# First stage of a fused attention and gated feed-forward kernel: merges, sums of squares and weight conversions at other places of a round

## The chip, the core and the metric

One core of one Trainium2 chip runs the whole program. The metric is the device time of one execution in microseconds (us); the kernel before was timed three times, with a median of 698.71 us (697.16 to 699.35). Engine names in the rows: PE is TensorE's matmul side and PEld its weight load, DVE is VectorE, ACT is ScalarE, POOL is GpSimd, and SP is the queue that issues the DMAs.

## What is computed

Causal attention over 4 batches, 12 heads, 448 positions and head size 64, then an RMS norm over the 768 joined channels and a gated feed-forward layer.

```
scores = q @ k.T / sqrt(64), causal mask, softmax over the keys
x      = (softmax @ v), heads side by side: 1792 x 768
xn     = x / sqrt(mean(x*x) + 1e-6) * rms_g
g, val = xn @ w_gate, xn @ w_val            # 768 -> 1536
out    = (g * sigmoid(g) * val) @ w_out     # 1536 -> 768
```

The weights arrive as 64-bit floats (`in_w`, an int64 view), and the kernel makes 32-bit floats of them itself.

## The kernel before, in words

**Tiles and groups.** A tile is a pair of heads of one batch with some of its queries (`UNITS`). Group 0 has 12 tiles of 256 queries (two for each of the six head pairs c), and this stage, from the start to about 69 us, is the one that the change touches. Two tiles of the same c fill one `xr` of 128 x 512.

**The order of work** is written out by hand. Every engine runs its own instructions in program order. The code walks through ticks (`tick`); a step of the schedule runs at each tick, and `post(n, f)` puts f off by n ticks. One round (`round_steps`) has six ticks and belongs to one tile p: scores of tile p+3, products of tile p with its values, then the two halves of the transposes of tile p+1, with two empty ticks between. The table `T` holds the delays: `exp0`, `norm0` and the like. What the steps issue:

- `scores` (L193, PE) into a `s_ps` bank; `softmax` takes the masked maximum from there (L202, DVE, four maxima for a tile, into `sp` and `nm`), three ticks later the exponentials (L205, ACT) and their sums `sm` (L227, ACT), and seven ticks later `norm`: the reciprocal `rs` (L214, DVE) and the four products sp times rs (L210, POOL; on ACT as L208 for the last two tiles of the group). These four are called the norms below.
- `some` transposes the norms' results (L249, PE) into `t_ps` and `x_ps`; the first half is copied to `pt` by ACT (L255), the second by DVE (L253).
- `products` (L275, PE) multiplies `pt` with the values `v_r`; `copy` brings the result to `xr` (L292, DVE).
- When the second tile of a head pair c is done, `square` (L300 on) makes the squares of its `xr`: on POOL through the helper at L103 for c = 0, 1, 2, on ACT (L308) for c = 3 and 4, on DVE (L310) for c = 5. The squares of c = 1 to 4 are then added to `acc` on DVE (L318), put off by `T["acc"]`. `split_x` makes `xh` (L335, ACT) and `xl` (L336, DVE).
- A weight unit of 128 x 768 is loaded (L395), and `convert_ops` puts its parts off from the tick in `CONVERT`: a scaled copy to `w_c` (L414, ACT, `c0`), a multiplication by zero of one half (L415, POOL, `c1`), the **first merge** (L417, DVE, `c20` in this stage), the **second merge** (L419, DVE, `c30`), and a store to DRAM (L421, SP, `c50`). At the tick in `SPLIT`, `split_w` makes `w_h` (L429, ACT) and `wl0`.. ticks later `w_l` (L431, DVE). The conversions come once in two rounds.
- `ffn_part` (L475 to L477, PE) multiplies finished `xh`, `xl` with finished `w_h`, `w_l`, some of it already between the rounds.
- At the end of the stage the squares are summed over the channels (L344, PE), first `acc`, then the squares of c = 5, and `rms_first` makes the scale from them: a square root (L353, ACT), a reciprocal, four diagonal blocks `dg` (L358, DVE), a matmul with ones (L362, PE) and a copy (L363, ACT).

**What waits for what, around the change:** the sum at L318 needs the squares; the maxima of the next tile stand behind it on DVE; the norms on POOL need `rs`, which stands behind those maxima.

In the table, `acc=3` puts the sum three ticks after the squares; conversions start at these ticks:

```
CONVERT = (20, 32, 44, 56, 62, 85)
SPLIT = (33, 45, 57, 70)
```

Of the kernel before, what the change touches and what calls it, by code (L numbers as in the profile page):

```python
# [10 lines left out]
F32 = mybir.dt.float32  # L11
# [11 lines left out]
P = 128  # L23
NP = H // 2
# [3 lines left out]
W = 512  # L28
# [10 lines left out]
        for g in range(NG) for c in range(NP)}  # L39
# [1 line left out]
MASKED = -8.0e9  # L41


T = dict(c0=0, c1=1, c2=4, c20=12, c3=4, c30=13, c26=5, c36=5, c5=6, c50=16, c56=7, exp=1, exp0=3, gt=1, hh=1, hl=4, ws=5, ld2=7,
         ld=4, ld1=11, lv=5, norm0=7, norm1=2, r0=1, acc=3, dg=1, spread=2, r1=5, so=3, wl=2, wl0=7, wl2=5, wl4=1, xl=2, xl0=9)
LOAD = (4, 12, 24, 36, 48, 60, 74, 86)
CONVERT = (20, 32, 44, 56, 62, 85)
SPLIT = (33, 45, 57, 70)

READY_W, READY_X = (45, 57, 68), (40, 52, 64, 76, 87)  # L50
WR = 4
# [11 lines left out]
def attention_ffn(ctx: ExitStack, tc: tile.TileContext, qk0, qk1, qk2, v, v2, w, g, out, out2):  # L63
# [11 lines left out]
    def pool(name, bufs, at=ctx, **kw):  # L75
        return at.enter_context(tc.tile_pool(name=name, bufs=bufs, **kw))
# [6 lines left out]
    ht_p = pool("ht", 4, ffn, side="left")  # L83
    rm_p = pool("rm", 1, ffn, side="left")
# [9 lines left out]
    def bank(tag, bufs=1):  # L94


        return ps.tile([P, W], F32, tag=tag, name=tag + "_ps", bufs=bufs)
# [4 lines left out]
    def pool_op(out_, a, op, b):  # L102
        nc.gpsimd.tensor_tensor(out_, a, b, op=op)  # L103
# [28 lines left out]
    def post(delay, fn):  # L132
        if delay <= 0:
            fn()
        else:
            later.setdefault(now[0] + delay, []).append(fn)
# [7 lines left out]
    xr, xh, xl, acc, xq = {}, {}, {}, {}, {}  # L144
# [6 lines left out]
    def load_qk(p):  # L151
        if p < len(UNITS):
            _, kind, _, _, row, _ = UNITS[p]
            raw_qk[p] = raw.tile([P, 2, W], F32, tag="qk", name="qk_r")
            if kind == 2:
                nc.sync.dma_start(out=raw_qk[p], in_=qk2[row])
            else:
                nc.sync.dma_start(out=raw_qk[p][:, 0], in_=(qk0, qk1)[kind][row])
# [14 lines left out]
    def steps_s(p):  # L173
# [22 lines left out]
        def softmax(e, i, pss):  # L196
            o, wd = bl[i]
            ps, sp = pss[e][:, o: o + wd], pr["sp"][e][:, o: o + wd]
            n = len(bl) * e + i
            nm, sm, rs = (pr[m][:, n: n + 1] for m in ("nm", "sm", "rs"))  # L200
            mk = mask2 if kind == 2 else mask[:, 3 * P - wd:]
            nc.vector.tensor_tensor_reduce(  # L202
                out=sp, in0=ps, in1=mk, scale=nsc, scalar=3.0e38,
                op0=ALU.add, op1=ALU.min, accum_out=nm)
            post(T["exp" if p >= ENDS[0] else "exp0"], lambda: nc.scalar.activation(  # L205
                sp, sp, AF.Exp, bias=nm, scale=-1.0, accum_out=sm))
            if ENDS[0] - 2 <= p < ENDS[1]:
                pr["norms"].append(lambda: nc.scalar.mul(sp, sp, rs))  # L208
            else:
                pr["norms"].append(lambda: nc.gpsimd.tensor_scalar(  # L210
                    sp, sp, rs, 1.0, op0=ALU.mult, op1=ALU.mult))
# [5 lines left out]
        def step():  # L217
# [6 lines left out]
            for e in range(2):  # L224
                for i in range(len(bl)):
                    softmax(e, i, pss)
            post(T["exp" if p >= ENDS[0] else "exp0"], lambda: nc.scalar.activation(  # L227
                pr["sm"][:, :nb], pr["sm"][:, :nb], AF.Identity, bias=tiny))
            post(T["norm1" if kind else "norm0"], norm)
            post(2, lambda: load_qk(p + 4))  # L230
# [68 lines left out]
    def square(b, c):  # L299

        halves = [(0, HX), (HX, XT)] if b == 2 else [(0, W)]
        for j, (lo, hi) in enumerate(halves):
            x = xr[b, c][:, lo: hi]
            sq = rm_p.tile([P, W], F32, tag="sq", name="sq") if c else \
                rm_p.tile([P, W], F32, tag="acc", name="acc", bufs=2)
            sq = sq[:, : hi - lo]
            if b or 2 < c < NP - 1:
                nc.scalar.activation(sq, x, AF.Square)  # L308
            elif c == NP - 1:
                nc.vector.tensor_tensor(sq, x, x, op=ALU.mult)  # L310
            else:
                pool_op(sq, x, ALU.mult, x)
            if c == 0:
                acc[b, j] = sq
            elif b:
                pool_op(acc[b, j], acc[b, j], ALU.add, sq)
            elif c < NP - 1:
                post(T["acc"], lambda: nc.vector.tensor_tensor(acc[0, 0], acc[0, 0], sq, op=ALU.add))  # L318
        if b == 2:
            return  # L320
        if c == NP - 1 and b:
            post(T["r1"], lambda: rms(b, [acc[b, 0]]))
        elif c == NP - 1:
            cols = column_sums(acc[b, 0], None, True)
            post(T["r0"], lambda: rms_first(column_sums(sq, cols, False)))
        waiting.append((b, c))

    def split_x():
        if not waiting:
            return  # L330
        b, c = waiting.pop(0)
        x, gc = xr[b, c], g_sb[:, c: c + 1]
        h = xx_p.tile([P, W], F32R, tag=f"xh{c}", name="xh")
        l = xx_p.tile([P, W], F32R, tag=f"xl{c}", name="xl")
        nc.scalar.mul(h, x, gc)  # L335
        post(T["xl0" if b == 0 and c < NP - 1 else "xl"], lambda: nc.vector.scalar_tensor_tensor(  # L336
            out=l, in0=x, scalar=gc, in1=f32(h), op0=ALU.mult, op1=ALU.subtract))
        xh[b, c], xl[b, c] = h, l

    def column_sums(sq, ps, first):  # L340

        ps = bank("t")[:, : W // P] if first else ps
        for i in range(W // P):
            nc.tensor.matmul(ps[:, i: i + 1], sq[:, P * i: P * (i + 1)], ones[:, :1],  # L344
                             start=first and i == 0, stop=not first, skip_group_check=True)
        return ps

    def rms_first(ps):

        rc = st_p.tile([P, W // P], F32, name="rc", bufs=1)  # L350
        dg = ht_p.tile([P, W], F32, tag="t", name="dg")
        r = rinv[0] = rm_p.tile([P, W], F32, tag="rms", name="rms", bufs=2)
        nc.scalar.activation(rc, ps, AF.Sqrt, bias=eps, scale=1.0 / DM)  # L353

        def diagonal():
            nc.vector.reciprocal(rc, rc)
            for i in range(W // P):
                nc.vector.tensor_scalar_mul(dg[:, P * i: P * (i + 1)], ident, rc[:, i: i + 1])  # L358

        def spread():  # L360
            ps = bank("t")
            nc.tensor.matmul(ps, ones, dg, start=True, stop=True)  # L362
            nc.scalar.copy(r, ps)  # L363

        post(T["dg"], diagonal)
        post(T["spread"], spread)

    def rms(b, parts):

        ps = bank("t")  # L370
        for i, sq in enumerate(parts):
            nc.tensor.matmul(ps, ones, sq, start=(i == 0), stop=(i == len(parts) - 1))
        r = rinv[b] = rm_p.tile([P, W], F32, tag="rms", name="rms", bufs=2)
        nc.scalar.activation(r, ps, AF.Sqrt, bias=eps, scale=1.0 / DM)
        for i in range(W // P):
            sl = slice(i * P, (i + 1) * P)
            post(i if b else 1, lambda sl=sl: nc.vector.reciprocal(r[:, sl], r[:, sl]))
# [46 lines left out]
    def split_w(s):  # L424
        if s < 2 * NU:
            t = wt[s]
            h = ws_p.tile([P, DM], F32R, tag="wh", name="w_h")
            l = ws_p.tile([P, DM], F32R, tag="wl", name="w_l")
            nc.scalar.copy(h, t)  # L429
            if s < NU or s > NU + 2 * NF and s % 2:  # L430
                post(T[("wl0", "wl0", "wl2", "wl2", "wl4")[s] if s < 5 else "wl"], lambda: nc.vector.tensor_tensor(l, t, f32(h), op=ALU.subtract))  # L431
            else:
                post(T["wl"], lambda: pool_op(l, t, ALU.subtract, f32(h)))
            wt[s] = tuple(a.rearrange("p (k m) -> p k m", m=P) for a in (h, l))
            u = s - NU
            if 0 <= u < 2 * NF:
                pair[u % 2] = t
                if u % 2:
                    post(T["ws"], lambda v=u // 2, t0=pair[0], t1=t: quad_sums(v, t0, t1))
# [400 lines left out]
    with tc.manual_schedule():  # L840
# [27 lines left out]

        for fs, at_ in ((load_w, LOAD), (lambda n: convert(n), CONVERT), (split_w, SPLIT)):
            for n, t_ in enumerate(at_):  # L870
# [14 lines left out]
        def convert(s):  # L885
            for d, op in convert_ops(s):
                post(d, op)
# [13 lines left out]
        for s in range(2 * NU):  # L901
# [15 lines left out]
            for k0 in (0, 2, 4):  # L917
# [7 lines left out]
                if i >= 73 and w_ == 0:  # L925
                    split_x()
                if k0 == (0 if s < 3 else 4) and s + 3 >= len(SPLIT):
                    split_w(s + 3)
                if k0 == 4 and s + 5 >= len(CONVERT):
                    convert(s + 5)  # L930
# [127 lines left out]
```

## Time and profile before

| | before |
|---|---|
| median of three runs | 698.71 us (697.16 to 699.35) |
| the profiled execution | 697.85 us, of which the span from first to last instruction is 696.0 us |
| busy share of the span | PE 97%, PEld 79%, DVE 77%, ACT 55%, POOL 43% |
| granted TensorE clock | 0.998 of full speed |

The span is one execution, read engine by engine. A timeline row gives the start, the length, the engine, the line, the operation and its output and input; in square brackets stands how long the engine had been idle before it and who ended that wait. A windows row gives the busy time of each engine in a stretch of the span. Busy times of neighbouring instructions overlap a little at their ends, so the time that an instruction adds to its queue is read from start to start.

### The profile page before, as it was taken

What the parts mean: (1) busy time and instruction counts of PE and PEld (TensorE: products, weight loads), DVE (VectorE), ACT (ScalarE), POOL (GpSimd) and SP (SyncE); (2) the same over time, 40 slices, a digit from 0 to 9 for tenths busy, and PEclk for the clock granted to TensorE, in tenths of its full rate; (3) what the DMA queues carried; (4) which work ended last, traced back from release to release, by engine and by line L of the source; (5) the groups of instructions that cost most, each with busy time, mean ns of one, the idle gap of its engine ahead of it and who ended that gap; (6) DMA issues with size and microseconds to landing.
All of it is one profiled execution on the core that took longest, in us unless ns stands there. A gap on an engine that the chain in (4) does not pass through costs nothing. (4 is left out here: it accounts for less than half of the span.)

```text
span 696.0 us, 11943 instructions
## 1 busy us (share of the span) xinstructions
PE 671.8 (97%) x4122; PEld 551.9 (79%) x4122; DVE 535.3 (77%) x1053; ACT 379.7 (55%) x856; POOL 298.6 (43%) x267
## 2 busy tenths in 40 slices
PE   8788989999999999999999999999899999999997
PEld 6456767777777767777777777888899999999997
DVE  4877989899988577777687878488386768679993
ACT  6885677888887446346354544445333433355550
POOL 4860212131225533756676566563254536312220
PEclk9999999999999999999999999999999999999999
DMA  8655688789879637576757655415457576553541
GB/s 264 201 201 172 189 254 256 218 259 285 258 218 343 228 117 233 169 238 211 266 159 263 198 174 170 153 60 177 156 189 246 172 247 217 200 151 89 168 139 69
DMA packets 71357, 138.82 MB, mean 199 GB/s; under 512 B 7744, under 2 KB 39232, under 8 KB 71296
## 3 DMA queue, kind: packets, MB, share of 16 engines
q1 hardware_dynamic: 71296, 138.05, 61.6%
q8 instruction: 33, 0.54, 0.3%
q14 instruction: 28, 0.23, 0.1%
HBM read 104.21 MB, written 33.82 MB: 198 GB/s over the span
## 5 line engine op out<-in xcount | busy, mean ns | idle before, releaser
L475 PE MATMUL m_ps<-xh,w_h 128*128 128x512 f32 x276 | 117.4, 425 | 2.5 <-DVE t_sb L502 2.5
L210 POOL TENSOR_SCALAR sp<-sp,rs 128x384 f32<-128x384 f32 (+2 forms) x112 | 78.3, 717 | 94.0 <-DVE rs L214 89.4
L205 ACT ACTIVATE sp<-sp,nm 128x384 f32<-128x384 f32 (+3 forms) x168 | 87.2, 521 | 39.6 <-DVE nm L202 39.6
L477 PE MATMUL m_ps<-xh,w_l 128*128 128x512 f32 x276 | 108.4, 393 | 0.0
L476 PE MATMUL m_ps<-xl,w_h 128*128 128x512 f32 x276 | 108.2, 392 | 0.0
L415 POOL TENSOR_SCALAR w<-w 128x768 f32<-128x768 f32 x36 | 38.6, 1073 | 112.5 <-ACT w_c L414 104.5
L103 POOL TENSOR_TENSOR a_l<-w_q,a_h 128x768 fp32r<-128x768 f32 x24 | 47.3, 1971 | 69.7 <-ACT a_h L516 69.6
L275 PEld LDWEIGHTS a_ps<-pt,v_r 128*64 128x64 f32 (+1 forms) x864 | 41.6, 137 | 38.5 <-DVE pt L253 10.9
L275 PE MATMUL a_ps<-pt,v_r 128*64 128x128 f32 (+2 forms) x864 | 60.0, 268 | 10.6 <-DVE pt L253 6.7
L475 PEld LDWEIGHTS m_ps<-xh,w_h 128*128 128x128 f32 x276 | 51.9, 188 | 14.8 <-issue 6.8
L103 POOL TENSOR_TENSOR w_l<-w_r,w_h 128x768 fp32r<-128x768 f32 x30 | 59.6, 1992 | 7.3 <-ACT w_h L429 7.2
L477 PEld LDWEIGHTS m_ps<-xh,w_l 128*128 128x128 f32 x276 | 51.8, 188 | 11.9
L253 DVE COPY pt<-t_ps 128x384 f32<-128x384 f32 (+1 forms) x71 | 42.4, 597 | 23.9 <-PE t_ps L249 23.4
L202 DVE CUSTOM_DVE_ANT_0 sp<-s_ps,mask 128x128 f32<-128x128 f32 (+3 forms) x136 | 49.9, 415 | 12.3 <-PE s_ps L193 11.1
L475 PE MATMUL m_ps<-hh,w_h 128*128 128x512 f32 x144 | 58.6, 407 | 0.0
L476 PEld LDWEIGHTS m_ps<-xl,w_h 128*128 128x128 f32 x276 | 52.2, 189 | 7.6
L477 PE MATMUL m_ps<-hh,w_l 128*128 128x512 f32 x144 | 56.2, 391 | 0.0
L476 PE MATMUL m_ps<-hl,w_h 128*128 128x512 f32 x144 | 56.2, 390 | 0.0
L249 PE MATMUL t_ps<-ident,sp 128*128 128x128 f32 (+1 forms) x309 | 50.1, 275 | 0.1
L249 PEld LDWEIGHTS t_ps<-ident,sp 128*128 128x128 f32 (+1 forms) x309 | 37.8, 137 | 14.3 <-issue 2.1
L193 PE MATMUL s_ps<-qk_r 64*128 64x128 f32 (+3 forms) x296 | 43.3, 421 | 1.7 <-DVE nm L202 1.5
L431 DVE TENSOR_TENSOR w_l<-w_c,w_h 128x768 fp32r<-128x768 f32 x36 | 40.3, 1120 | 3.9 <-ACT w_h L429 3.9
(196 smaller groups left out, 1678.6 us busy)
## 6 DMA issues: line engine op xcount, KB each, us to landing
w<-in_w SPq DMA_DIRECT2D x36, 768.0 KB, 5.1
w<-w_c SPq DMA_DIRECT2D x36, 384.0 KB, 5.7
w_r<-w SPq DMA_DIRECT2D x36, 384.0 KB, 4.8
qk_r<-in_qk SPq DMA_DIRECT2D x48, 256.0 KB, 4.7
qk_r<-in_qk SPq DMA_DIRECT2D x12, 512.0 KB, 5.6
v_r<-in_v SPq DMA_DIRECT2D x12, 448.0 KB, 5.0
v_r<-in_v SPq DMA_DIRECT2D x24, 192.0 KB, 3.4
wy<-w_r SPq DMA_DIRECT2D x24, 192.0 KB, 4.4
```

The costliest lines, as they stand in the source:

```text
L103: nc.gpsimd.tensor_tensor(out_, a, b, op=op)
L193: nc.tensor.matmul(ps, r[:, q0: q0 + nq], r[:, k0: k0 + wd], start=True, stop=True)
L202: nc.vector.tensor_tensor_reduce(out=sp, in0=ps, in1=mk, scale=nsc, scalar=3.0e38, op0=ALU.add, op1=ALU.min, accum_out=nm)
L205: post(T["exp" if p >= ENDS[0] else "exp0"], lambda: nc.scalar.activation(sp, sp, AF.Exp, bias=nm, scale=-1.0, accum_out=sm))
L210: pr["norms"].append(lambda: nc.gpsimd.tensor_scalar(sp, sp, rs, 1.0, op0=ALU.mult, op1=ALU.mult))
L249: nc.tensor.transpose(ps[:kb, at: at + P], pr["sp"][e][:, o + kb * j: o + kb * (j + 1)], ident)
L253: nc.vector.tensor_copy(pt[:kb, :at], ps[:kb, :at])
L275: nc.tensor.matmul(av_ps[e * D: (e + 1) * D, p % 2, q0: q0 + n], raw_v[p][:kb, h, j, e, :], pr["pt", e][:kb, a0: a0 + n], start=(j == 0), ...
L431: post(T[("wl0", "wl0", "wl2", "wl2", "wl4")[s] if s < 5 else "wl"], lambda: nc.vector.tensor_tensor(l, t, f32(h), op=ALU.subtract))
L475: nc.tensor.matmul(ps, wh[:, k, :], mh, start=(first and k == ks[0]), stop=False)
L476: nc.tensor.matmul(ps, wh[:, k, :], ml, start=False, stop=False)
L477: nc.tensor.matmul(ps, wl[:, k, :], mh, start=False, stop=(last and k == 5))
```

## The change

It changes four delays and two lists of ticks in the schedule's tables, the engine of one square, and the pool of one buffer.

```diff
-T = dict(c0=0, c1=1, c2=4, c20=12, c3=4, c30=13, c26=5, c36=5, c5=6, c50=16, c56=7, exp=1, exp0=3, gt=1, hh=1, hl=4, ws=5, ld2=7,
-         ld=4, ld1=11, lv=5, norm0=7, norm1=2, r0=1, acc=3, dg=1, spread=2, r1=5, so=3, wl=2, wl0=7, wl2=5, wl4=1, xl=2, xl0=9)
+T = dict(c0=0, c1=1, c2=4, c20=16, c3=4, c30=18, c26=5, c36=5, c5=6, c50=19, c56=7, exp=1, exp0=3, gt=1, hh=1, hl=4, ws=5, ld2=7,
+         ld=4, ld1=11, lv=5, norm0=7, norm1=2, r0=1, acc=10, dg=1, spread=2, r1=5, so=3, wl=2, wl0=7, wl2=5, wl4=1, xl=2, xl0=9)
-CONVERT = (20, 32, 44, 56, 62, 85)
-SPLIT = (33, 45, 57, 70)
+CONVERT = (14, 26, 38, 50, 62, 85)
+SPLIT = (34, 46, 58, 70)
@@ square
-            if b or 2 < c < NP - 1:
+            if b or c == NP - 2:
                 nc.scalar.activation(sq, x, AF.Square)
@@ rms_first
-        dg = ht_p.tile([P, W], F32, tag="t", name="dg")
+        dg = rm_p.tile([P, W], F32, tag="sq", name="dg")
```

The first merge of a unit moves from tick 12 to tick 16 after its conversion's start, the second from 13 to 18, the store from 16 to 19, and the sum of squares from 3 to 10 ticks after the squares. The first four conversions start six ticks (one round) sooner, three of the splits one tick later. The squares of c = 3 go from ACT to POOL. The diagonal blocks `dg` use the buffer of the squares and no longer one of the four buffers of `ht_p`. TensorE's order is the same, instruction for instruction.

**VectorE, around the sum of squares.** Before, the end of one round and the first maximum of the next tile (w_l is the low part of a weight unit, w_290 and w_383 are raw weight units):

```order
L214 RECIPROCAL rs<-sm 128x4
L292 COPY xr<-a_ps 128x256
L431 TENSOR_TENSOR w_l<-w_c,w_h 128x768
L253 COPY pt<-x_ps 128x384
L318 TENSOR_TENSOR acc<-acc,sq 128x512
L202 ISA sp,nm<-s_ps,mask 128x128
```

After, the same round, from the last maximum of its own tile to the first maximum of the next:

```order
L202 ISA nm 128x1
L318 TENSOR_TENSOR acc<-acc,sq 128x512
L214 RECIPROCAL rs<-sm 128x4
L292 COPY xr<-a_ps 128x256
L431 TENSOR_TENSOR w_l<-w_c,w_h 128x768
L253 COPY pt<-x_ps 128x384
L417 SCALAR_TENSOR_TENSOR w_383<-w_383 128x768
L202 ISA sp,nm<-s_ps,mask 128x128
```

The sum has gone from ahead of a tile's maxima to behind them, and takes the squares of a pair of rounds earlier; the first merge of the next unit has come in ahead of the maxima.

**VectorE, the other round of the pair.** Before, both merges stand side by side:

```order
L214 RECIPROCAL rs<-sm 128x4
L292 COPY xr<-a_ps 128x256
L417 SCALAR_TENSOR_TENSOR w_290<-w_290 128x768
L419 SCALAR_TENSOR_TENSOR w_c<-w_c,w_290 128x768
L253 COPY pt<-x_ps 128x384
L336 SCALAR_TENSOR_TENSOR xl<-xr,g_sb,xh 128x512
```

After, only the second is left there:

```order
L214 RECIPROCAL rs<-sm 128x4
L292 COPY xr<-a_ps 128x256
L419 SCALAR_TENSOR_TENSOR w_c<-w_c,w_383 128x768
L253 COPY pt<-x_ps 128x384
L336 SCALAR_TENSOR_TENSOR xl<-xr,g_sb,xh 128x512
L202 ISA sp,nm<-s_ps,mask 128x128
```

The copy `pt` that TensorE's products wait for has one merge ahead of it in place of two.

**GpSimd, one pair of rounds.** Before (sp_482, sp_536, sp_537, ... are the score blocks of successive tiles, w64 a raw weight unit):

```order
L415 TENSOR_SCALAR w64_383<-w64_383 128x768
L210 TENSOR_SCALAR sp_536<-sp_536,rs_535 128x128
L210 TENSOR_SCALAR sp_536<-sp_536,rs_535 128x256
L210 TENSOR_SCALAR sp_537<-sp_537,rs_535 128x128
L210 TENSOR_SCALAR sp_537<-sp_537,rs_535 128x256
L103 TENSOR_TENSOR sq_634<-xr_557 128x512
L210 TENSOR_SCALAR sp_597<-sp_597,rs_596 128x128
```

After:

```order
L210 TENSOR_SCALAR sp_539<-sp_539,rs_538 128x128
L210 TENSOR_SCALAR sp_539<-sp_539,rs_538 128x256
L210 TENSOR_SCALAR sp_540<-sp_540,rs_538 128x128
L210 TENSOR_SCALAR sp_540<-sp_540,rs_538 128x256
L103 TENSOR_TENSOR sq_636<-xr_560 128x512
L415 TENSOR_SCALAR w64_493<-w64_493 128x768
L210 TENSOR_SCALAR sp_596<-sp_596,rs_595 128x128
```

Before, a square follows one tile's norms and a multiplication of a weight unit the other's; after, both follow the same tile's norms.

On SP the store of a unit (L421) comes one row sooner, ahead of a load of values (L167) in place of behind it.

## Rows read from the trace of the kernel before

**Rows 1.** Busy time by stretch: stretch in us, its length, each engine's busy us (instructions).
```profile
18.75:29.20 10.45, 8.86 (x61) 5.54 (x57) 8.19 (x27) 10.04 (x32) 9.16 (x12) 1.00 0.75 253
29.20:39.32 10.12, 8.12 (x50) 5.30 (x51) 8.10 (x28) 7.45 (x24) 7.86 (x10) 1.00 0.58 192
39.32:49.21 9.89, 8.42 (x53) 5.40 (x52) 8.10 (x28) 7.63 (x25) 7.72 (x10) 1.00 0.57 197
49.21:62.38 13.17, 9.54 (x54) 5.91 (x52) 10.48 (x25) 10.35 (x26) 0.88 (x1) 1.00 0.61 205
...
69.09:160.00 90.91, 87.29 (x442) 66.35 (x441) 84.48 (x158) 71.05 (x171) 19.65 (x18) 1.00 0.77 239
```

**Rows 2.** Timeline of DVE, from one sum of squares to the next.
```profile
28.60 0.69 DVE L318 TENSOR_TENSOR acc<-acc,sq 128x512 f32<-128x512 f32 x1 [1.98 <-POOL sq L103]
29.20 0.28 DVE L202 CUSTOM_DVE_ANT_0 sp<-s_ps,mask 128x128 f32<-128x128 f32 x1
...
30.31 0.17 DVE L214 RECIPROCAL rs<-sm 128x4 f32<-128x4 f32 x1
30.40 0.39 DVE L292 COPY xr<-a_ps 128x256 f32<-128x256 f32 x1
30.71 0.95 DVE L417 SCALAR_TENSOR_TENSOR w<-w 128x768 int32<-128x768 int32 x1
31.70 0.96 DVE L419 SCALAR_TENSOR_TENSOR w_c<-w_c,w 128x768 int32<-128x768 int32 x1
32.57 0.55 DVE L253 COPY pt<-x_ps 128x384 f32<-128x384 f32 x1
33.04 0.84 DVE L336 SCALAR_TENSOR_TENSOR xl<-xr,g_sb,xh 128x512 fp32r<-128x512 f32 x1
33.81 0.28 DVE L202 CUSTOM_DVE_ANT_0 sp<-s_ps,mask 128x128 f32<-128x128 f32 x1
...
35.32 0.94 DVE L431 TENSOR_TENSOR w_l<-w_c,w_h 128x768 fp32r<-128x768 f32 x1
36.18 0.55 DVE L253 COPY pt<-x_ps 128x384 f32<-128x384 f32 x1
38.71 0.69 DVE L318 TENSOR_TENSOR acc<-acc,sq 128x512 f32<-128x512 f32 x1 [1.99 <-POOL sq L103]
```

**Rows 3.** Timeline of POOL in the same pair, and one undisturbed set of norms before it.
```profile
13.83 1.62 POOL L210 TENSOR_SCALAR sp<-sp,rs 128x128 f32<-128x128 f32 x4 [0.97 <-DVE rs L214]
...
30.66 3.57 POOL L210 TENSOR_SCALAR sp<-sp,rs 128x128 f32<-128x128 f32 x4 [2.10 <-DVE rs L214]
34.20 0.89 POOL L415 TENSOR_SCALAR w<-w 128x768 f32<-128x768 f32 x1
35.25 2.42 POOL L210 TENSOR_SCALAR sp<-sp,rs 128x128 f32<-128x128 f32 x4 [0.15 <-DVE rs L214]
37.64 1.04 POOL L103 TENSOR_TENSOR sq<-xr 128x512 f32<-128x512 f32 x1
```

**Rows 4.** Timelines of POOL and DVE at 118 us, where two of these operations meet.
```profile
118.49 1.15 POOL L415 TENSOR_SCALAR w<-w 128x768 f32<-128x768 f32 x1 [2.61 <-ACT w_c L414]
118.82 1.63 DVE L431 TENSOR_TENSOR w_l<-w_c,w_h 128x768 fp32r<-128x768 f32 x1
```

**Rows 5.** Timeline of DVE: one copy ahead of the maxima that start at 18.75 us.
```profile
17.79 0.56 DVE L253 COPY pt<-x_ps 128x384 f32<-128x384 f32 x1 [0.27 <-PE x_ps L249]
```

**Rows 6.** DMA issues at 6, 26 and 44 us: size and us from issue to landing.
```profile
w<-in_w SPq DMA_DIRECT2D x1, 768.0 KB, 5.1
...
v_r<-in_v SPq DMA_DIRECT2D x1, 128.0 KB, 4.2
...
v_r<-in_v SPq DMA_DIRECT2D x1, 128.0 KB, 6.2
```

**Rows 7.** Timeline of DVE at the end of group 0.
```profile
60.87 0.56 DVE L253 COPY pt<-x_ps 128x384 f32<-128x384 f32 x1 [1.77 <-PE x_ps L249]
...
62.38 0.42 DVE L292 COPY xr<-a_ps 128x256 f32<-128x256 f32 x1 [0.30 <-PE a_ps L275]
```

## The prediction, made before the changed kernel ran

> **What bounds the kernel now.** I read busy time by stretch first. Behind 69 us TensorE is busy nearly all the time (87.29 of 90.91 us), while in the stage that the change touches it is not: the three pairs of rounds between 18.75 and 49.21 us take 10.45, 10.12 and 9.89 us, 30.46 together, and no engine's work needs that [rows 1]. The exception is the first of them, where ScalarE is busy for 10.04 us.
>
> Then the timelines of a pair. VectorE stands still for 1.98 and 1.99 us ahead of the sum of squares, until GpSimd's squares are there [rows 2]. GpSimd in turn stands still for 2.10 us ahead of its next norms, until VectorE's reciprocal is there [rows 3]. Together they make a ring: norms 30.66 to 34.20, the multiplication of a unit, norms from 35.25, squares until 38.68 [rows 3], then on VectorE the sum from 38.71, the maxima, the reciprocal, and the next norms. GpSimd's part is 3.57 + 0.89 + 2.42 + 1.04 = 7.92 us, end to end about 8.0; the sum with the maxima (28.60 to 30.31, 1.71) and the step to GpSimd at 30.66 add 2.1. That is the pair's 10.1 us. The reader is to see that the wait is no lack of speed in an engine: the maxima need nothing from the squares and stand behind a sum that does.
>
> **The sum of squares behind the maxima.** It takes 0.60 us from start to start wherever it stands [rows 2], so its own time is no gain. What goes is the ring: the squares that it takes now were made a pair of rounds earlier. The 2.0 us of VectorE and the 2.1 us of GpSimd go together, being one wait seen from both ends. What is late next are the engines' lists, per pair:
>
> - VectorE, start to start [rows 2]: maxima 1.11 twice, reciprocal and copy 0.40 twice, first merge 0.99, second 0.87, `pt` 0.47 twice, `xl` 0.77, `w_l` 0.86, sum 0.60: 8.05 us.
> - TensorE: busy 8.12 and 8.42 us [rows 1]; matmuls that wait inside are counted whole, so this is an upper end.
> - ScalarE: 7.45 and 7.63 us [rows 1].
> - GpSimd: four norms take 1.62 us alone, 2.42 with one two-input VectorE operation right behind the reciprocal (`w_l`), and 3.57 with both merges and `xl` there [rows 3]. Now one merge follows each reciprocal at most, so I take 2.42 twice: 2 x 2.42 + 0.89 + 1.04 = 6.77. The other end is 3.57 twice, 9.07.
>
> **The two merges apart.** Their 0.99 and 0.87 us stay in VectorE's list. The copy `pt` that releases TensorE's products has one merge less ahead of it. In return the first merge now starts in the middle of a set of norms, and the second near the squares. What such a meeting costs is seen once outside the stage: GpSimd's 1.15 us multiplication had started at 118.49, and VectorE's `w_l`, begun at 118.82, took 1.63 us in place of 0.94 [rows 2, 4], so 0.69 more. In the stage itself `xl` runs beside the norms that are there now and takes 0.84, which is counted above. Two or three of the five two-input operations of a pair will meet something; the norms are short. Bounds: 0, and 0.69 for each of five, 3.45. I take 0.4 to 0.5, nearest to the rows of the stage itself, and so **8.5 us for a pair**, just above TensorE's 8.42.
>
> Three pairs: 30.46 - 25.5 = **5.0 us won**. At VectorE's bare 8.05 it would be 6.3.
>
> **Start of the stage.** The conversions begin a round sooner. The first merge now stands behind the copy of 17.79 [rows 5] and ahead of the maxima that started at 18.75; 0.4 us of its 0.95 fit into VectorE's wait there, and the rest delays those maxima: 17.79 + 0.47 + 0.95 = 19.2. **Cost 0.4 us.** ScalarE's scaled copy of the first unit comes before the third tile's exponentials now. The load takes 5.1 us [rows 6], and its lead is a round shorter now, so ScalarE may stand there for some tenths. Bounds 0 and 0.95, a pass over the same block by VectorE [rows 2]; I take 0, since the first tiles' other work there waits for loads of values anyway, and keep 0.95 for the range.
>
> **End of the stage**, 49.21 to 62.38 us. One first merge (0.99) leaves this stretch for the one ahead of it, and one sum (0.60) comes in later than before, behind `xl` and before the last copy of `xr`. VectorE waits here for TensorE's transposes (1.77) and products (0.30) [rows 7], which themselves wait for copies behind merges, so an earlier merge is felt; ScalarE, busy 10.35 of 13.17 us [rows 1], keeps it from more. Bounds 0 and 1.4 (0.99 and a part of the waits); I take **0.9 won**.
>
> **Other edits.** The squares of c = 3 add 1.04 us to GpSimd [rows 3] where it does next to nothing afterwards (0.88 us of work in 49.21 to 62.38 [rows 1]), since the last two tiles' norms are ScalarE's; covered, 0. If GpSimd should be late there, the sum behind `xl` would wait up to those 1.04. `dg` in the squares' buffer must wait until TensorE has read the squares of c = 5; its own input comes from that very product, so 0. On SP, a load of values is now queued behind a store that waits for the second merge. In the list above that merge ends 6.7 us after the pair's first maximum (1.11 + 0.60 + 0.40 + 0.86 + 0.47 + 0.9 + 1.11 + 0.40 + 0.87), and the products that need these values come behind the next pair's first `pt`, at 8.5 + 3.4, which leaves about 5 us; loads of values took 4.2 us, and 6.2 right behind a 768 KB weight load [rows 6], which now comes after them. I take 0.
>
> **Carrying on.** Every engine works in order, and behind 69 us TensorE is the limit; the rest of the program moves forward as a block. The sum: 5.0 - 0.4 + 0.9 = 5.5 us, from the profiled 697.85 to 692.35. That execution was 0.86 us below the median of the runs, so **693.2 us** for the median.
>
> **Rivals.**
> (a) *GpSimd becomes the bound.* If both sets of norms are held as long as the worst is now, its list is 9.07 us, without any idle time. For: 3.57 is what three held norms cost [rows 3]. Against: only one merge follows each reciprocal now. Three pairs 27.2, won 3.3, less 0.4 at the start: 695.8 for the median. Chance 0.15.
> (b) *The gain is eaten by a late load of values.* If loads behind the store take 6.2 us, products wait 1.2 us in each pair and the first waits more; with GpSimd or ScalarE late as well (10.04 of 10.45 us busy in the first pair [rows 1]), a pair is back near 9.9. Won 0.8 in three, less 0.4 at the start, and nothing at the end: about 698.3. Chance 0.11. That the edits do not move the wait at all belongs here, 0.02 more; the new order speaks against it.
> (c) *Slower: VectorE is held by GpSimd.* In the old order VectorE's two-input operations start right behind the reciprocal, as GpSimd's norms begin, and win. In the new one they start while GpSimd is at work. If each of the five in a pair loses 0.69 us [rows 4], the list is 8.05 + 3.45 = 11.5, 1.35 more than now, 4.0 in three pairs, and with 0.4 at the start the median is about 703. It decides from (10.15 - 8.05) / 5 = 0.42 us for each operation. Against: eight of GpSimd's ten operations in a pair are norms of 0.4 us each (1.62 for four [rows 3]), and a chance meeting costs about half of one. Chance 0.06. The Trainium skill, "SBUF — State Buffer", section "SBUF: two separate sides", says that VectorE, with two SBUF inputs, and a GpSimd operation that reads SBUF share a port pair under an exclusive lock: who starts first has it for the whole instruction, and the other is blocked. The meeting at 118 us agrees with that, the loser there being VectorE.
>
> **Chances and range.** The forecast (pairs of 8.05 to 8.8 us) has 0.66. A difference of 0.3%, 2.1 us, is about what a measurement of this kernel can tell from none, so faster means under 696.6. Forecast and (a) lie there: with a little of (b), 0.82. The same: 0.12. Slower: 0.06. Low end: 8.05 a pair (6.3) with the whole 1.4 at the end and 0.4 at the start give 7.3, 691.4, and 0.4 less if the start costs nothing: 691.0. High end: through (a), with 0.95 more for ScalarE at the start: 696.8. What is left out is (c) and most of (b).
>
> **What would show it.** Right: no idle time of note ahead of the sum of squares; sets of maxima two rounds apart by 8.0 to 8.8 us; GpSimd's 2.10 us before a set of norms gone; the last copy of `xr` near 57 us; the stretches behind 69 us as long as now. Wrong: VectorE's merges, `w_l` or `xl` at 1.3 us and more (c); sets of norms at 3.5 us and GpSimd without idle time (a); TensorE's products released by a DMA (b); or a shorter stage followed by new idle time of TensorE.

## The result, and the profile after

| | before | after |
|---|---|---|
| median, four runs each | 698.91 us (697.16 to 699.35) | 691.64 us (689.42 to 692.87) |
| ratio, 95% interval | | 0.9897 [0.9864, 0.9930] |
| once more, nine runs and five | 698.43 us | 689.92 us, 0.9891 [0.9871, 0.9911] |
| profiled execution, its span | 697.85, 696.0 us | 690.72, 688.9 us |

The changed kernel is 7.3 us faster in the first comparison, 8.5 in the second. The forecast was 693.2, from 691.0 to 696.8: the first median lies inside, the repeat 1.1 us below the low end.

Busy time by stretch of the kernel after: the three pairs of rounds from the first maxima, the end of group 0 up to the last copy of `xr`, then the stretch behind the stage. Columns are those of [rows 1].

```profile
19.21:27.59 8.38, 6.90 (x45) 3.66 (x45) 8.12 (x27) 8.17 (x29) 7.71 (x11) 1.00 0.62 200
27.59:36.11 8.52, 7.89 (x52) 4.73 (x51) 8.52 (x28) 7.44 (x25) 7.72 (x11) 1.00 0.78 277
36.11:44.32 8.21, 7.83 (x55) 5.28 (x54) 8.21 (x28) 6.90 (x23) 8.21 (x11) 1.00 0.67 222
44.32:57.09 12.77, 10.50 (x61) 6.98 (x60) 10.87 (x26) 10.98 (x28) 4.53 (x5) 1.00 0.63 208
65.44:160.00 94.56, 90.88 (x460) 69.11 (x458) 88.06 (x161) 74.25 (x177) 20.89 (x19) 1.00 0.78 237
```

Pairs that took 10.45, 10.12 and 9.89 us [rows 1] take 8.38, 8.52 and 8.21, with VectorE busy without a gap in the second and third. Its timeline in the kernel after, for the counterpart of [rows 2]:

```profile
28.70 0.17 DVE L214 RECIPROCAL rs<-sm 128x4 f32<-128x4 f32 x1
28.79 0.39 DVE L292 COPY xr<-a_ps 128x256 f32<-128x256 f32 x1
29.10 1.08 DVE L419 SCALAR_TENSOR_TENSOR w_c<-w_c,w 128x768 int32<-128x768 int32 x1
30.10 0.55 DVE L253 COPY pt<-x_ps 128x384 f32<-128x384 f32 x1
30.57 0.91 DVE L336 SCALAR_TENSOR_TENSOR xl<-xr,g_sb,xh 128x512 fp32r<-128x512 f32 x1
...
32.51 1.00 DVE L318 TENSOR_TENSOR acc<-acc,sq 128x512 f32<-128x512 f32 x1
...
33.83 0.94 DVE L431 TENSOR_TENSOR w_l<-w_c,w_h 128x768 fp32r<-128x768 f32 x1
34.70 0.54 DVE L253 COPY pt<-x_ps 128x384 f32<-128x384 f32 x1
35.16 1.02 DVE L417 SCALAR_TENSOR_TENSOR w<-w 128x768 int32<-128x768 int32 x1
```

The sum at 32.51 waits for nothing; the 1.99 us ahead of it are gone. POOL in the same pair, for [rows 3]:

```profile
25.24 3.12 POOL L210 TENSOR_SCALAR sp<-sp,rs 128x128 f32<-128x128 f32 x4 [0.67 <-DVE rs L214]
28.33 1.04 POOL L103 TENSOR_TENSOR sq<-xr 128x512 f32<-128x512 f32 x1
29.34 1.60 POOL L415 TENSOR_SCALAR w<-w 128x768 f32<-128x768 f32 x1
30.90 2.06 POOL L210 TENSOR_SCALAR sp<-sp,rs 128x128 f32<-128x128 f32 x4
33.76 3.12 POOL L210 TENSOR_SCALAR sp<-sp,rs 128x128 f32<-128x128 f32 x4 [0.80 <-PE x_ps L249]
```

Where GpSimd stood 2.10 us for the reciprocal, it now waits 0.67 for it, or 0.80 for TensorE's transposes. One meeting shows: the multiplication at 29.34 starts 0.24 us after VectorE's second merge and takes 1.60 us in place of 0.89 [rows 3]; here GpSimd is the one that is held.

**Where the time went.** The two profiled spans differ by 7.1 us. Cut at four instructions that both have (the first maxima, the last copy of `xr`, the first `gr` at L492, the last output block `ob` at L486):

| stretch | before | after | won |
|---|---|---|---|
| start to first maxima | 18.75 | 19.21 | -0.46 |
| to the last copy of `xr` | 43.63 | 37.88 | 5.75 |
| to the first `gr` | 6.71 | 8.35 | -1.64 |
| to the last `ob` | 419.86 | 420.17 | -0.31 |
| to the end | 207.05 | 203.29 | 3.76 |

Two large rows of this table were not in the prediction's sum, the third and the last. The third first; the timeline of all engines of after, end of the stage:

```profile
55.15 0.74 DVE L336 SCALAR_TENSOR_TENSOR xl<-xr,g_sb,xh 128x512 fp32r<-128x512 f32 x1
55.44 1.18 POOL L415 TENSOR_SCALAR w<-w 128x768 f32<-128x768 f32 x1 [7.78 <-ACT w_c L414]
55.81 1.35 DVE L318 TENSOR_TENSOR acc<-acc,sq 128x512 f32<-128x512 f32 x1
57.09 0.41 DVE L292 COPY xr<-a_ps 128x256 f32<-128x256 f32 x1
57.31 1.02 PE L344 MATMUL t_ps<-ones,acc 128*128 128x1 f32 x8 [1.15 <-DVE acc L318]
...
61.83 2.02 PE L362 MATMUL t_ps<-dg,ones 128*128 128x512 f32 x2
65.44 0.69 DVE L492 TENSOR_TENSOR gr<-m_ps,rms 128x512 f32<-128x512 f32 x1 [1.93 <-PE m_ps L477]
```

The last sum, of c = 4, now stands just ahead of the last copy of `xr`, meets a GpSimd multiplication, and takes 1.35 us in place of 0.69. TensorE's column sums (L344) wait 1.15 us for it; in e3 and e5 below the sum stands at the same place, nothing holds it (0.68 us), and they wait 0.60 and 0.61. Three microseconds after the wait the clock falls; the stretch in a windows view of after:

```profile
60.60:64.00 3.40, 3.40 (x7) 1.79 (x6) 2.74 (x6) 0.12 (x1) 0.00 (x0) 0.50 0.01 2
```

The granted clock is 0.50, 1.2 in place of 2.4 GHz, for 3.4 us, so about 1.7 us of work are lost; the matmul with ones at 61.83 takes 2.02 us, where it takes 1.10 at full clock. From the column sums to the first `gr` it is 8.13 us here, 7.10 in e9 below, whose clock stays at 1.00, and 6.81 before: about 1.0 us of the row goes with the clock. Before the fall TensorE had waited those 1.15 us and worked on from 57.31. In the profile of the kernel before the same stage has no such stretch; it has one elsewhere, which leads to the last row of the table. The timeline of before behind its last `ob`, and the window that follows:

```profile
488.95 0.69 DVE L486 SCALAR_TENSOR_TENSOR ob<-m_ps,rms 128x512 f32<-128x512 f32 x1 [4.33 <-PE m_ps L477]
490.50 0.43 SPq L488 DMA_DIRECT2D out_t<-ob  x1
494.05 0.48 ACT L648 COPY m<-m_ps 128x384 f32<-128x384 f32 x1 [4.77 <-DMA out_t<-ob]
494.58 0.44 PE L625 MATMUL m_ps<-ch,a_h 128*128 128x384 f32 x1 [2.54 <-ACT m L648]
```

```profile
495.80:499.20 3.40, 3.40 (x13) 3.40 (x12) 2.41 (x2) 2.70 (x4) 1.97 (x2) 0.50 0.26 62
```

The same place in after:

```profile
485.61 0.69 DVE L486 SCALAR_TENSOR_TENSOR ob<-m_ps,rms 128x512 f32<-128x512 f32 x1 [4.55 <-PE m_ps L477]
487.17 0.43 SPq L488 DMA_DIRECT2D out_t<-ob  x1
487.18 0.48 ACT L648 COPY m<-m_ps 128x384 f32<-128x384 f32 x1 [1.24 <-PE m_ps L625]
491.11 0.56 DVE L653 TENSOR_TENSOR u<-m,s_ps 128x384 f32<-128x384 f32 x1 [4.34 <-ACT t L662]
```

L648 is the first copy of the second feed-forward part (`m1`, in a pool that is opened when those of the first part are closed, so in their memory). Before, it waited until the last output block had been stored, TensorE waited 2.54 us for the copy, and in this execution the clock fell to 0.50 behind that (e2 below has the same wait without the fall). After, the copy waits for TensorE alone. ScalarE's order of instructions is the same at this place; the semaphores that the copy waits for are not. Before, then after:

```order
L648 COPY m_5643<-m_ps 128x384 [waits DMAHW0_49,DVE_49,PE_49]
```

```order
L648 COPY m_5643<-m_ps 128x384 [waits DMAHW3_49,PE_49]
```

So the memory that `m1` takes over belonged to the last `ob` before, and to an earlier one now. What shifted it: `dg` no longer takes one of the four buffers "t" of `ht_p`, in which `gr`, `ob` and others go round. With one user fewer ahead of them, each later one lies one buffer further back.

### The profile page after: what moved, and what is told of

Same layout as the page of the kernel before. It is cut to its first block, busy times and chain, and to the rows that moved or that the text cites. A ratio compares the mean times of both kernels' runs of the same rounds, so it can differ in the third digit from the quotient of the medians.

```text
span 688.9 us, 11941 instructions
## 1 busy us (share of the span) xinstructions
PE 671.3 (97%) x4122; PEld 551.2 (80%) x4122; DVE 536.5 (78%) x1053; ACT 378.2 (55%) x855; POOL 301.0 (44%) x268
## 5 line engine op out<-in xcount | busy, mean ns | idle before, releaser
L415 POOL TENSOR_SCALAR w<-w 128x768 f32<-128x768 f32 x36 | 41.1, 1143 | 109.9 <-ACT w_c L414 101.8
```

## The experiments

Theory: the gain in the stage (5.35 us in its three pairs) comes from the sums behind the maxima, and the gain behind 485 us from `dg` alone. Rivals: that the new places of merges and conversions make the gain, or that it is one effect carried along. In the table, "first `gr`" and "tail" (last `ob` to end) come from each kernel's one profiled execution, "clock" is the mean granted clock over its timed runs.

| run | median us | ratio [95%] | first `gr` | tail | clock |
|---|---|---|---|---|---|
| e1_dg | 695.18 | 0.9961 [0.9945, 0.9977] | 70.38 | 204.5 | 0.994 |
| e2_nodg | 693.10 | 0.9929 [0.9906, 0.9952] | 65.08 | 206.5 | 0.997 |
| e3_acc | 694.54 | 0.9953 [0.9932, 0.9974] | 65.87 | 206.2 | 0.996 |
| e4_noacc | 696.94 | 0.9969 [0.9951, 0.9988] | 72.14 | 206.0 | 0.994 |
| e5_acc_dg | 691.19 | 0.9902 [0.9885, 0.9918] | 64.84 | 203.6 | 0.998 |
| e6_lastob | 690.71 | 0.9893 [0.9875, 0.9911] | 65.07 | 204.8 | 0.997 |
| e7_c4early | 687.79 | 0.9856 [0.9837, 0.9876] | 62.33 | 204.0 | 1.000 |
| e8_after | 689.92 | 0.9891 [0.9871, 0.9911] | 64.67 | 203.1 | 0.997 |
| e9_c4early | 689.50 | 0.9879 [0.9857, 0.9900] | 62.54 | 205.5 | 1.000 |
| e10_sqact | 688.93 | 0.9872 [0.9852, 0.9892] | 62.66 | 202.4 | 1.000 |
| e11_short | 689.66 | 0.9886 [0.9868, 0.9904] | 64.90 | 203.1 | 1.000 |
| e12_pair | 693.67 | 0.9945 [0.9925, 0.9965] | 66.60 | 206.1 | 0.998 |

The kernel before had 698.53 beside the first four, 698.43 beside the next four, 697.54 beside the last, and a mean clock of 0.994 in these 46 runs.

### `dg` alone (e1), and everything but `dg` (e2)

```diff
# e1: the kernel before with
-        dg = ht_p.tile([P, W], F32, tag="t", name="dg")
+        dg = rm_p.tile([P, W], F32, tag="sq", name="dg")
# e2: the changed kernel with that line as before
```

> The kernel before with one edit: the diagonal blocks in the squares' buffer. Theory A (the change has two gains: the ring in the first stage, and this buffer, which shifts the ring of four output buffers by one, so that ScalarE's first copy at the start of the second feed-forward part no longer waits 4.77 us for the last output store): the first stage is as before (last copy of xr near 62.4 us, sum of squares waiting about 2.0 us), TensorE's idle 2.54 us near 494 is gone, and the time is 2.5 to 4.2 us less, 694.7 to 696.4. Rival B (all of the gain is the schedule of the first stage, and what differs near 494 is scatter between executions): no difference from before, 698.9, and the wait of 4.77 us still there.

> The changed kernel with the diagonal blocks back in their old buffer. Theory A: the first stage as in the changed kernel (pairs of 8.2 to 8.6 us), the copy near 488 waits over 4 us for the output store, and the time is 694 to 696. Rival B: 691.6, like the changed kernel.

`dg` alone wins 3.35 us and nothing in the stage (its first `gr` is even later than before, 70.38 against 69.09, in a profile whose clock fell at 54.7 us). The copy of e1:

```profile
491.93 0.48 ACT L648 COPY m<-m_ps 128x384 f32<-128x384 f32 x1 [1.24 <-PE m_ps L625]
496.33 0.55 DVE L653 TENSOR_TENSOR u<-m,s_ps 128x384 f32<-128x384 f32 x1 [4.81 <-DMA out_t<-ob]
```

The wait for the store has moved to VectorE's `u`, four microseconds on. There it costs less, but not always nothing: VectorE then works without a gap until TensorE waits 1.09 us for it at 500.78 in e1, while in after TensorE does not wait at all from 480 to 520 us. In e2 it is back at the old place, at a stage that is as short as the changed kernel's:

```profile
490.13 0.48 ACT L648 COPY m<-m_ps 128x384 f32<-128x384 f32 x1 [4.81 <-DMA out_t<-ob]
490.66 0.45 PE L625 MATMUL m_ps<-ch,a_h 128*128 128x384 f32 x1 [2.58 <-ACT m L648]
490.66:506.00 15.34, 15.34 (x88) 15.34 (x89) 10.54 (x15) 9.09 (x14) 7.33 (x4) 1.00 0.59 185
```

The last line is a windows row: behind this wait the clock stays at 1.00, and the tail is 206.5 us all the same. So the fall seen before is not what makes most of the 3.76 us behind the last `ob`. The schedule without `dg` is worth 5.43 us (698.53 - 693.10); the time is 0.9 us below the range expected. Both halves of the theory hold: the stage keeps its gain without `dg`, and the wait comes and goes with `dg`.

### The sums alone (e3), and everything but the sums (e4)

```diff
# e3: the kernel before with
-... norm0=7, norm1=2, r0=1, acc=3, ...
+... norm0=7, norm1=2, r0=1, acc=10, ...
# e4: the changed kernel with acc=3
```

> The kernel before with the sum of squares ten ticks behind the squares in place of three, nothing else. If the ring (sum waiting for squares, maxima behind the sum) is what the first stage loses: no wait ahead of the sum, pairs of 8.5 to 9.3 us with both merges still ahead of the copy pt, 3 to 4.5 us less than before, 694.4 to 696. Rival (the merges' places or the earlier conversions make the gain): pairs stay over 9.8 us, 698 or more.

> The changed kernel with the sum of squares at its old three ticks. If the ring is the cause, it closes again: VectorE waits ahead of the sum and the first stage loses 3 to 5 us, 694.5 to 697. As the squares now come right behind one tile's norms, the sum may be ready sooner; if the merges' places are the cause of the gain, under 693.

The sums alone win 3.99 us, and no sum waits for its squares any more. VectorE in e3:

```profile
32.67 0.72 DVE L318 TENSOR_TENSOR acc<-acc,sq 128x512 f32<-128x512 f32 x1
41.20 0.72 DVE L318 TENSOR_TENSOR acc<-acc,sq 128x512 f32<-128x512 f32 x1
```

Its pairs take 7.99, 8.53 and 8.52 us, as short as the changed kernel's, with both merges still side by side ahead of one copy. Everything but the sums wins 1.59 us, less than `dg` alone (3.35). By the medians, merges and conversions by themselves would cost about 1.8 us; the intervals of e1 and e4 overlap, so that is not shown. The profile of e4, of the slowest of its twelve runs (699.64 us), points the same way: pairs of 11.44, 10.47 and 10.40 us. VectorE in e4:

```profile
29.43 1.34 DVE L318 TENSOR_TENSOR acc<-acc,sq 128x512 f32<-128x512 f32 x1 [1.73 <-POOL sq L103]
39.87 1.37 DVE L318 TENSOR_TENSOR acc<-acc,sq 128x512 f32<-128x512 f32 x1 [0.93 <-POOL sq L103]
50.28 1.36 DVE L318 TENSOR_TENSOR acc<-acc,sq 128x512 f32<-128x512 f32 x1 [1.73 <-POOL sq L103]
```

and POOL in e4:

```profile
29.37 0.86 POOL L415 TENSOR_SCALAR w<-w 128x768 f32<-128x768 f32 x1
39.81 0.88 POOL L415 TENSOR_SCALAR w<-w 128x768 f32<-128x768 f32 x1
50.22 0.88 POOL L415 TENSOR_SCALAR w<-w 128x768 f32<-128x768 f32 x1
```

The ring of norms, squares, sum and maxima is still there, and the multiplication that now follows the squares starts 0.06 us ahead of each sum, which then takes 1.34 to 1.37 us in place of 0.69. That is the meeting of rival (c), three times, in a kernel that has a half of the change.

### Sums and `dg` together (e5), the last block elsewhere (e6)

```diff
# e5: the kernel before with both edits of e1 and e3
# e6: the changed kernel with
-            ob = ht_p.tile([P, W], F32, tag="t", name="ob")
+            ob = rm_p.tile([P, W], F32, tag="acc", name="ob", bufs=2) if s == 2 * NU - 1 else \
+                ht_p.tile([P, W], F32, tag="t", name="ob")
```

> The kernel before with two edits: the sum of squares at ten ticks and the diagonal blocks in the squares' buffer; merges, conversions, splits and the squares of c = 3 as before. Theory A (two separate gains that add, the merges' places worth little): 3.99 + 1.5 to 3.35 us less than before, 691.2 to 693.1, so within 1.5 us of the changed kernel. Rival (the merges' new places carry a good part): 694 or more.

> The changed kernel, with the last output block of the first feed-forward part written into a buffer of the sums of squares in place of the ring of four, so that what first takes its memory afterwards is a later operation (the fifth after ScalarE's copy). In the changed kernel VectorE's first sum there waits for the last output store. Theory A (that store's landing is on the path): VectorE's sum starts within 1 us after ScalarE's copy, TensorE has no idle time over 0.3 us from 480 to 520 us, and the time is 0 to 1.5 us below the changed kernel in this call. Rival B (scatter only): no change in the waits' length and the same time.

The parts add up: 3.35 + 3.99 = 7.34, and e5 measured 7.24. What is left for merges, splits, conversions and the squares of c = 3 is the distance to e8, 1.27 us, and the two intervals overlap. The profiles see more between these two: from the third pair to the last copy of `xr` 14.02 us in e5 and 12.74 in e8, of which 0.9 is given back up to the first `gr`. e6 takes the last store out of everyone's way: VectorE's sum starts 1.1 us behind ScalarE's copy, in after 3.45. TensorE still waits once, 1.10 us at 506.27, for what stands behind loads of weights, and the time is not below e8's (690.71 and 689.92). So with `dg` moved, no cost of that wait can be seen.

### The last sum sooner (e7, and again as e9), the changed kernel once more (e8)

```diff
# e7, e9: the changed kernel with
-                post(T["acc"], lambda: nc.vector.tensor_tensor(acc[0, 0], acc[0, 0], sq, op=ALU.add))
+                post(T["acc"] if c < NP - 2 else 3, lambda: nc.vector.tensor_tensor(acc[0, 0], acc[0, 0], sq, op=ALU.add))
```

> The changed kernel with only the last of the four sums (c = 4) at its old three ticks: it comes ahead of the next to last copy of xr, no longer behind xl, where it took 1.35 us because GpSimd held it and TensorE waited 1.15 us for it. Expected: TensorE's wait ahead of the column sums gone, the column sums 0.5 to 1.1 us sooner, the time 0.3 to 1.1 us below the changed kernel in this call. Rival: the chain there is ScalarE's (square root, copy), then no gain.

> The changed kernel itself once more, on the same chip as the three beside it: 691 to 692.5 us. It is the measure for the other three; if the 1.5 us between the changed kernel and the one with the old diagonal buffer is real, it stays below 692.5.

> The changed kernel with the last sum of squares put back to 3 ticks, once more, as the base of the three runs beside it. If the gain over the changed kernel (689.92 to 687.79) is TensorE's wait of 1.15 us ahead of the column sums and the stretch at half the clock that followed it (3.41 us at half, 1.7 lost), it repeats: 687.5 to 688.3, with no such wait and no such stretch near 60 us. If the 2.1 us were luck of that run: about 690.

The end of the stage in e9, timeline of all engines:

```profile
55.44 1.05 PE L344 MATMUL t_ps<-ones,acc 128*128 128x1 f32 x8
59.94 1.10 PE L362 MATMUL t_ps<-dg,ones 128*128 128x512 f32 x2 [0.36 <-DVE dg L358]
62.54 0.69 DVE L492 TENSOR_TENSOR gr<-m_ps,rms 128x512 f32<-128x512 f32 x1 [0.88 <-PE m_ps L477]
```

and the window that answers to 60.60 to 64.00 above:

```profile
58.00:62.54 4.54, 4.18 (x17) 2.79 (x17) 2.97 (x8) 1.16 (x3) 0.00 (x0) 1.00 0.12 40
```

TensorE no longer waits ahead of the column sums, the clock stays at 1.00, and the first `gr` comes at 62.54 and 62.33 against 64.67 in e8. Of the 2.34 us between e7 and e8, 1.34 lie ahead of the column sums (55.23 against 56.57) and 1.00 behind them (7.10 us to the first `gr` in place of 8.10). In all ten runs of e7 and e9 the mean granted clock is 0.999 or 1.000; in the nine of the changed kernel (e8 and the first comparison) 0.994 to 0.998, but for one at 1.000.

The time itself is less sure. e7 is 2.13 us below e8, more than the 0.3 to 1.1 expected. e9, expected at 687.5 to 688.3, measured 689.50, close to the 690 that was written down for luck. Counted from the kernel before beside each, e7 won 10.64 us, e9 8.04 and the changed kernel itself 8.51 (e8, 1.1 us below its expected range), and the intervals of the three overlap. So the wait and the slow stretch go both times; that the whole program is then faster than the changed kernel is not shown.

### What the other edits are worth on that base (e10, e11, e12)

```diff
# e10: e9 with the squares of c = 3 on ScalarE
-            if b or c == NP - 2:
+            if b or 2 < c < NP - 1:
# e11: the kernel before with the edits of e1, e3 and e7 alone
# e12: e9 with both merges side by side
-... c20=16, c3=4, c30=18, ... c50=19 ...
+... c20=12, c3=4, c30=13, ... c50=16 ...
```

> The kernel of the run beside it with the squares of c = 3 on ScalarE, as before the change. The prediction gave that edit nothing: then the time is that of the run beside it within 0.5 us. If ScalarE is what holds the end of the stage (10.35 of 13.17 us busy there before), its 0.5 to 0.6 us more make the last copy of xr later by up to that, 0.6 us slower. If GpSimd's squares of c = 3 cost VectorE something by the shared port: up to 0.7 us faster.

> The kernel before with three edits alone: the sums of squares behind the maxima (10 ticks), the last of them at 3, and dg in the squares' buffer; merges, conversions, splits and the squares of c = 3 as they were. Theory one, that merges and conversions at their new places are worth the 1.3 us by which the changed kernel stood below the same sums and dg without them: about 689.1, 1.3 above the run with everything. Theory two, that those 1.3 us are TensorE's wait and clock at the end of the stage and not the merges: the same as the run with everything, within 0.5.

> The run with everything, its two merges side by side again, at 12 and 13 ticks (store at 16), with the conversions half a round sooner kept. Both merges and w_l then stand in the same round of a pair, ahead of one copy pt, and the other round has xl alone. If the place of the merges matters, because TensorE's products wait for that copy: one round of a pair is longer by up to 0.9 us and the other shorter only by what VectorE was its limit, so 0.5 to 0.9 us per pair, 1.5 to 2.5 us slower in all. If the sum's place is all that counts: within 0.5 us of the run with everything.

e10: 0.57 us faster than e9, no difference that can be told; in the profile the first `gr` is 0.12 us later, so the prediction's 0 for this edit stands. e11, with three edits, is as fast as e9 with all of them (689.66 and 689.50), which is theory two's number. Its profile says something else: the first `gr` comes 2.36 us later, 2.1 counted from the first maxima, so in the stage the other edits do win, at its end (from the third pair to the last copy of `xr` 13.68 us in e11 and 11.87 in e9; the three pairs together 25.01 and 24.83). The tail of e9 is longer by as much. e12 is 4.2 us slower than e9, more than either theory gave: its first `gr` is 4.06 us later, 2.0 of it in the pairs, as the first theory had it, 1.5 at the end of the stage and 0.6 ahead of the first maxima. TensorE's waits in e12:

```profile
27.43 0.86 PE L275 MATMUL a_ps<-pt,v_r 128*64 128x256 f32 x6 [1.41 <-DVE pt L253]
36.54 0.86 PE L275 MATMUL a_ps<-pt,v_r 128*64 128x256 f32 x6 [2.14 <-DVE pt L253]
46.43 0.86 PE L275 MATMUL a_ps<-pt,v_r 128*64 128x256 f32 x6 [2.24 <-DVE pt L253]
```

Both merges and `w_l` stand ahead of one copy `pt` in every second round; the second and third pairs are 9.10 and 9.89 us again although the sum waits for nothing. So it is not that the merges must stand apart (in e11 they do not): the three long operations must not fall into one round. Of the places tried here, the change's earlier conversions go with its separated merges only.

**The tail's scatter.** Between kernels that differ in the stage alone, the tail runs from 202.4 to 206.1 us. One part of it shows in VectorE's timeline, first in e10, then in e12:

```profile
500.83 1.17 DVE L685 TENSOR_TENSOR wq<-wq 128x768 f32<-128x768 f32 x1 [0.44 <-DMA wq<-w]
```

```profile
507.11 0.96 DVE L685 TENSOR_TENSOR wq<-wq 128x768 f32<-128x768 f32 x1 [2.72 <-DMA wq<-w]
```

VectorE, in order, waits for four loads of weights; in e12 TensorE then waits 1.75 us for what stands behind. That is 18.2 and 20.5 us after the last `ob` of each. Whether an earlier stage makes these loads land later, or it is chance, these runs do not settle; with it, e9 and e11 can't be told apart.

## Why the prediction was right, and where it was not

**Pairs of 8.5 us: right.** Measured 8.38, 8.52 and 8.21, together 5.35 us won where the text had 5.0. The place of the sums is the cause: alone it gives pairs of 7.99, 8.53 and 8.52 us (e3), and without it the rest of the change gives 10.40 and more (e4). The ring was drawn a little too simply: ahead of the third pair's sum VectorE had waited 1.76 us for ScalarE's squares (48.60 us), not for GpSimd's. VectorE's list is what bounds, as worked out, its two-input operations stretched by little (`w_l` 0.94, first merge 1.02, second 1.08, `xl` 0.91, one sum 1.00). GpSimd came closer to the bound than I had it: 3.12 + 2.06 for the norms, 1.04, and 1.60 in place of 0.89 make 7.8 us where the text had 6.77.

**Start, 0.4 us lost: the delay is there, its cost in time can't be told.** The first merge holds up the first maxima as worked out: from the start of the copy ahead of both to the maxima it is 1.49 us in both profiles of the changed kernel (17.72 to 19.21, and 17.29 to 18.78 in e8), and 0.96 before. But that copy itself starts at another time in each execution, and over the fourteen profiles the first maxima start between 17.94 and 19.43 us, old and new places mixed.

**End of the stage, 0.9 won: 0.40** (13.17 to 12.77 us), and 1.64 given back behind it. That earlier merges are felt here was right, and more than the 0.9: 1.8 us between e11 and e9, whose sums stand at the same places. The step that failed is "one sum (0.60) comes in later than before, behind `xl` and before the last copy of `xr`": it counted the sum's own time and not who waits. TensorE's column sums do, for 1.15 us, and a clock of 0.50 came behind that. e7 and e9 take the sum away from there, and both go.

**"`dg` in the squares' buffer ... so 0": wrong, and the largest miss.** I looked at the buffer that it enters and not at the ring that it leaves. Measured 3.35 us alone, and 1.5 to 3.2 as the distance from e2 to the changed kernel's two medians. Against the total: 5.5 us predicted, 5.43 measured for the schedule, 7.3 to 8.5 with `dg`. That the first median lies in the range is luck in part: in the two profiles, 3.76 us won behind the last `ob` were not in the sum, and against them stand 2.45 us that it did not expect to lose (0.50 at the end of the stage, 1.64 behind it, 0.31 up to the last `ob`).

**Squares of c = 3, values, SP: 0, right.** No wait for `v_r` shows in the stretch, and e10 has the squares.

**Carrying on one to one: right** from the first `gr` to the last `ob` (419.7 to 420.2 us in all fourteen profiles), not behind it.

**Rivals.** (a) GpSimd as the bound at 9.07 us: no, though in the third pair it is busy for all of 8.21 us. (b) Products released by a load: no. (c) VectorE held by GpSimd: the mechanism is real, its count is not. In the changed kernel one sum (55.81, 1.35) and part of another lose time, not five operations in each pair; from e4 one sees where it would have cost. The Trainium skill, "SBUF — State Buffer", section "SBUF: two separate sides", describes the lock as held for a whole instruction by whoever starts first. The traces agree with that on both sides: e4's sums lose, 0.06 us behind GpSimd (1.34 to 1.37 us in place of 0.69), and after's multiplication at 29.34 loses, 0.24 us behind VectorE (1.60 in place of 0.89).

## What to carry to other kernels

When an accumulation stands ahead of the next tile's critical operation, put it behind, and look who consumes the last one: give that one a place of its own, if the profile shows its consumer waiting. When a buffer is taken out of a rotating pool, every later user moves by one; follow the ring to its end, and into whatever reuses its memory. Operations that are harmless one by one must be spread so that no single round holds all of them ahead of what TensorE waits for.

## What was not expected of the hardware

The clock answers to small changes of the schedule. The mean granted clock rose from 0.994 (46 runs of the kernel before) to 0.997 (nine of the changed one) and 1.000 (22 runs of e7, e9, e10 and e11, all 0.999 or 1.000), and in the two profiles shown it falls 1.2 and 3.3 us behind the end of a wait of TensorE of over a microsecond. It is not that each such wait brings a fall. Before, TensorE waits 1.68 us for `pt` at 53.20 and the clock stays; in e1 it falls at 54.7 behind the same wait (1.66 us at 53.70). Behind the wait for the output store it fell before and not in e2, and of e3 and e5, which both wait 0.6 us ahead of the column sums, it falls in e3 alone. e12, whose last sum also comes early, has a mean of 0.998 and a fall near 510 us, behind a wait of 1.75 us at 508.59. Nor does each fall cost time: over the 46 runs of the kernel before, its clock (0.990 to 0.999) and its time are not related. What makes the clock fall stays open.
